# Packed attention with a routed MLP: token order of the key probabilities, the value load, and the queue that loads tau

## The chip, the cores and the metric

The kernel runs on one core of a Trainium2 chip. The metric is the device time of one execution in microseconds; less is better. The kernel before was run three times: 432.28 us in the median, 431.61 to 433.13. All times below are microseconds (us) unless marked ns.

## The reference

Eight batches of eight heads, 576 tokens of width 64. Per head, 32 pack queries `p` attend to the keys and values, and the tokens' own queries `q` then attend to the 32 packed rows. The result, 512 wide per token, goes through a mixture of eight experts of which each token uses one.

```python
def sm_attn(qq, kk, vv):
    s = scale * np.matmul(qq, kk.transpose(0, 1, 3, 2))
    s = s - np.max(s, axis=-1, keepdims=True)
    a = np.exp(s)
    a = a / (np.sum(a, axis=-1, keepdims=True) + 1e-09)
    return np.matmul(a, vv)
p_packed = sm_attn(p, k, v)              # 32 x 576 scores per head
out = sm_attn(q, p_packed, p_packed)     # 576 x 32 scores per head
...
logits = xn @ en.T / tau                 # x and the embeddings, each divided by its norm
expert_idx = np.argmax(logits, axis=1)
...
h = np.maximum(x[mask] @ w1[e], 0.0)
out[mask] = gate_w[mask, None] * (h @ w2[e])
```

## The kernel before

The batches go through one after the other, and two of them overlap: while TensorE does the expert MLP of batch b (`ffn`: lines 930, 958 and 976), pieces of the attention of batch b + 1 are put in between (`att1`, `att2`, `route`, `gates`). The order is written out by hand: `PLAN` says for batch 0 which piece follows each step of the MLP, and from batch 1 on a fixed rule advances the next batch's generator once per step. Each engine works through its own list in that order. Batch 0 has a start of its own, `begin`, with nothing to overlap it: it loads p, the embeddings, keys, values, queries and tau, does the first attention and guesses one expert for the whole batch; w1 and w2 of that expert are loaded after the guess (`load_w1`, `load_w2`). A loop at the end handles tokens that the guess misses.

The parts that the change touches:

- **Keys and queries.** A head's 576 tokens lie as 32 partitions of 18 neighbouring tokens each. `load_whole` (line 189, batch 0) loads four heads in one DMA, `load_nat` (line 174, later batches) two heads in four DMAs of 32 partitions. `flip` turns them in blocks of 32 x 32 on VectorE, so that column 32 n + i of `kt` is token 18 i + n. For queries that is one instruction (line 289). For keys it is three (lines 284 to 286), which also permute the blocks n. Each group of four heads has two flips at the start, one for each half of the width, and each later batch has four flips of keys and four of queries. A flip in `begin` is followed by `quarters` (line 237), the scores of that group.
- **Key softmax.** `key_max` (line 344, VectorE) and `key_exp` (line 349, ScalarE) make 128 x 576 probabilities `p1` of a group of four heads from PSUM; `p1` has the columns in the order of the scores. `p1_turn` (line 364) turns them on TensorE in five pieces, four of 128 columns and one of 64, each a weight load of the piece and a matmul with the identity; `p1_evac` copies the result out, and `pack_values` (line 384) multiplies by the values.
- **Values.** `load_v` (line 200) loads four heads. Partition 32 a + i holds tokens 18 i + n for the run of n that `RUNS` gives to the band a, five or four of them, so that piece c of `p1` meets the same tokens. Each band is a DMA of its own: 32 partitions, four heads, 1280 or 1024 bytes at a time.
- **tau.** One number, copied to 128 partitions of `itau` by a DMA of GpSimd's software queue (line 1096), issued behind the other loads in the program. Its reciprocal (line 1137) scales the logits.
- **Embeddings.** `embeddings` is a generator whose steps (norms by a Newton rsqrt, partly on VectorE, mostly on GpSimd) `begin` advances between its own.

Tiles of keys, queries and values share six buffers (`nat`). SP issues nearly all loads and stores, in program order.

Of the kernel before, what the change touches and what calls it, by code (L numbers as in the profile page):

```python
# [13 lines left out]
AF = mybir.ActivationFunctionType  # L14
# [3 lines left out]
P = 128  # L18
HB = 4
# [4 lines left out]
def kernel(  # L24
# [12 lines left out]
    nc = tc.nc  # L37
    B, H, S, D = q.shape
# [3 lines left out]
    NPR = H // 2  # L42
    NF = F // P
    HS = S // 2
    NCB = S // 32
# [23 lines left out]
    for h in range(HB):  # L69
        nc.vector.memset(pairs[32 * h : 32 * h + 32, h // 2 : h // 2 + 1], 1.0)  # L70
        for g in range(NG):
            at = (h ^ g) % 2
# [47 lines left out]
    itau = cp.tile([P, 1], F32, name="itau")  # L120
# [64 lines left out]
    def load_whole(src, g):  # L185

        t = sb.tile([P, NC5 * HB * D], F32, name="nat", tag="nat", bufs=6)[:, : NCB * D]
        s = src[0, g * HB : (g + 1) * HB].rearrange("h (i c) d -> h i (c d)", c=NCB)
        nc.sync.dma_start(t, s.rearrange("h i w -> (h i) w"))
        return t  # L190


    RUNS = ((0, 5), (5, 5), (10, 4), (14, 4))

    def load_v(b, g):
        t = sb.tile([P, NC5 * HB * D], F32, name="nat", tag="nat", bufs=6)
        t = t.rearrange("p (h w) -> p h w", h=HB)
        s = v[b, g * HB : (g + 1) * HB].rearrange("h (i c) d -> i h (c d)", c=NCB)
        for a, (at, n) in enumerate(RUNS):
            nc.sync.dma_start(  # L200
                t[32 * a : 32 * a + 32, :, : n * D], s[:, :, at * D : (at + n) * D]
            )
        return t.rearrange("p h (c d) -> p h c d", c=NC5)

    def load_p(b, queue=nc.sync):
# [9 lines left out]
    def rows(c):  # L215
        return P if c < 4 else 64
# [56 lines left out]
        nc.scalar.copy(dst[0], src)  # L273
        eng.tensor_tensor(out=dst[1], in0=src, in1=dst[0].bitcast(F32), op=ALU.subtract)

    def flip(t, key, e=0):

        kt = sb.tile([P, S], F32, name="kt", tag="kq", bufs=8)
        t = t.rearrange("p (c e d) -> p c e d", e=2, d=32)[:, :, e]
        if key:  # L280

            ko = kt[:, :512].rearrange("p (n a i) -> p a n i", a=4, i=32)
            ti = t[:, :10].rearrange("p (a n) d -> p a n d", a=2)
            nc.vector.transpose(ko[:, :2], ti[:, :, :4])
            nc.vector.transpose(ko[:, 2:], t[:, 10:].rearrange("p (a n) d -> p a n d", a=2))
            nc.vector.transpose(kt[:, 512:].rearrange("p (a i) -> p a i", i=32), ti[:, :, 4])
        else:

            nc.vector.transpose(kt.rearrange("p (n i) -> p n i", i=32), t)  # L289
        return kt  # L290

    def packers(x, pn):

        x.pw = sm.tile([P, NPR, 32], F32, name="pw", tag="pw", bufs=1)
        nc.vector.tensor_scalar_mul(pn, pn, SCALE)
        nc.vector.transpose(
            x.pw.rearrange("p r j -> p (r j)"), pn.rearrange("p r d -> p (r d)")
        )

    def keys(x, nat, pn):  # L300

        packers(x, pn)
        yield
        for r in range(NPR):
            x.kT[r] = flip(nat(r), True)
            yield


# [30 lines left out]
    def s1_view(x, g):  # L339
        return x.s1[g].rearrange("p (f s) -> p f s", f=2)[:, :, :HS]  # L340
# [5 lines left out]
    def key_exp(x, g):  # L346
        x.p1[g] = sb.tile([P, S], F32, name="p1", tag="p1", bufs=2)
        x.sums[g] = sm.tile([P, 1], F32, name="sums", tag="sums")
        nc.scalar.activation(
            x.p1[g].rearrange("p (f s) -> p f s", f=2), s1_view(x, g), AF.Exp, bias=x.mx[g],  # L350
            accum_out=x.sums[g],
        )

    def key_sum(x, g):
# [6 lines left out]
    def p1_turn(x, g, pt, pl):  # L361
        for c in range(NC5):
            r = rows(c)
            nc.tensor.transpose(  # L364
                (pt[:r, c * P : (c + 1) * P] if c < 4 else pl[:r, :P]),
                x.p1[g][:, c * P : c * P + r],
                ident,
            )

    def p1_evac(x, g, pt, pl, w=512, spare=None):  # L370

        x.p1T[g] = sb.tile([P, NC5, P], F32, name="p1T", tag=spare or "p1T", bufs=NF if spare else 2)
        t = x.p1T[g][:, 0:4].rearrange("p a b -> p (a b)")
        if w:
            nc.scalar.copy(t[:, :w], pt[:, :w])
        if w < 512:
            nc.vector.tensor_copy(t[:, w:], pt[:, w:512])
        nc.vector.tensor_copy(x.p1T[g][:64, 4], pl[:64, :P])
# [27 lines left out]
    def pair_rows(x, g, pt):  # L406
        x.pp2[g] = masked(x, g, pt, mask2[g], 2, "pp2")

    def packed_rows(x, g, pt):
        nc.scalar.mul(x.ppf[:, g, :D], pt[:, 0:D], x.rinv[g])  # L410
# [6 lines left out]
    def pack_tiles(x):  # L417
        x.T = x.Tq = sm.tile([P, NG * P], F32, name="T", tag="T", bufs=1)
        x.ppf = sb.tile([P, NG, XW], F32, name="ppf", tag="ppf", bufs=2)
# [15 lines left out]
    def att1(x, nat, tight=False):  # L435

        def queries():
            for r in range(NPR):
                x.qT[r] = flip(nat(NPR + r), False)
                yield  # L440

        turned = []

        def turn(g):
            turned.append(pb.tile([P, 1024], F32, name="pt", tag="pb"))
            p1_turn(x, g, turned[g], turned[g][:, 512:])

        def evac(g, w=512):
            p1_evac(x, g, turned[g], turned[g][:, 512:], w)

        def values():
            pt = pb.tile([P, 1024], F32, name="pt", tag="pb")
            for g in range(NG):
                pack_values(x, g, nat(2 * NPR + g), pt[:, g * D : g * D + D])
            return [pt[:, g * D : g * D + D] for g in range(NG)]

        def pack():
            pack_tiles(x)
            if not tight:
                yield  # L460
            for g in range(NG):
                turn(g)
            for g in range(NG):
                evac(g, 0 if tight and g else 512)
                if not tight:
                    yield
            if tight:
                yield
            pts = values()
            if not tight:  # L470
                yield
            for g in range(NG):
                pair_rows(x, g, pts[g])
            if not tight:
                yield
            pu = ps.tile([P, 512], F32, name="pu", tag="pf")
            if tight:
                for g in range(NG):
                    packed_rows(x, g, pts[g])
                yield  # L480
            for g in range(NG):
                pair_turn(x, g, pu)
            if not tight:
                yield
            (nc.scalar.copy if tight else nc.vector.tensor_copy)(x.T, pu[:, 0 : NG * P])
            if tight:
                yield
            else:
                for g in range(NG):
                    packed_rows(x, g, pts[g])  # L490
                yield from idle(2)
            pt = ps.tile([P, 512], F32, name="pu", tag="pf")
            row_logits(x, pt)
            if not tight:
                query_scores(x)
                yield
            logits_out(x, pt, nc.scalar.copy if tight else nc.vector.tensor_copy)
            yield

        key_scores(x)  # L500
        if tight:
            x.queries = queries()
        yield
        if tight:
            for g in range(NG):
                key_max(x, g)
            yield
            for g in range(NG):
                key_exp(x, g)
                key_sum(x, g)  # L510
                yield
            yield from pack()
            return
        for g in range(NG):
            key_max(x, g)
            yield
            key_exp(x, g)
            key_sum(x, g)
            yield
        yield from alternate(pack(), queries())  # L520
# [563 lines left out]
    def begin():  # L1084
# [3 lines left out]
        x = bat[0]  # L1088
        emb_gen = embeddings()
        pn = sm.tile([P, NG, D], F32, name="pn4", tag="pn")  # L1090
        nc.scalar.dma_start(pn, p[0].rearrange("(g h) j d -> (h j) g d", g=NG))
        next(emb_gen)
        kn = [load_whole(k, g) for g in range(NG)]
        vn = [load_v(0, g) for g in range(NG)]
        qn = [load_whole(q, g) for g in range(NG)]
        nc.gpsimd.dma_start(itau, tau.broadcast_to([P, 1]))

        def bank():
            return ps.tile([P, 512], F32, name="pf", tag="pf")
# [20 lines left out]
        for g in range(NG):  # L1120
            x.s1[g] = turn_bank()
            for e in range(2):
                kt = flip(kn[g], True, e)
                for hf in range(2):
                    quarters(x.s1[g], pw[:, 1, g, e], kt, lambda c: head(g, c), hf, hf, e)
            next(emb_gen)
            if g == 0:
                next(emb_gen)
        prefetch(1)
        key_max(x, 0)  # L1130
# [76 lines left out]
        for g in range(NG):  # L1207
            at = NG * 2 * D + g * NCB * D
# [180 lines left out]
    with tc.If(n_rest > 0):  # L1389
        with tc.For_i(0, B, 1) as b:  # L1390
            nb = nc.values_load(rest_i[0:1, ds(b, 1)], min_val=0, max_val=S)
            with tc.If(nb > 0):
                x = Batch()
                pn = load_p(b)
                nat = lambda i: load_nat(b, i)
# [96 lines left out]
```

## Time and profile before

| what | value |
|---|---|
| median of three runs | 432.28 us |
| the profiled execution | 434.17 us |
| its span, from the first instruction to the last | 432.5 us |
| TensorE matmuls busy (PE) | 416.7 us, 96% |
| weight loads busy (PEld; they overlap PE) | 349.6 us, 81% |
| VectorE busy (DVE) | 311.9 us, 72% |
| ScalarE busy (ACT) | 217.5 us, 50% |
| GpSimd busy (POOL) | 139.5 us, 32% |
| DMA, mean | 204 GB/s |

The profile is of one execution. In the rows further down, a row of the timeline has the start in us, the busy time in us, the engine, the line, the operation with out<-in and the shapes, and in brackets how long the engine had been idle and what ended that. SPq, ACTq and POOL rows with DMA_DIRECT2D are the issue of a DMA, not its transfer.

### The profile page before, as it was taken

The page shows a single profiled execution, that of the slowest core. Times are in us where ns is not written, and L with a number is a line of the kernel's source. Part 1 is how long each engine was busy: PE and PEld are TensorE (multiplying, and loading weights), DVE is VectorE, ACT ScalarE, POOL GpSimd, SP SyncE. Part 2 cuts the span into 40 slices and gives each one's busy share as a digit, 9 for nine tenths or more (in the row PEclk, how much of TensorE's full clock was granted, in tenths as well). Part 3 has the DMA queues.
Part 4 walks back from the last instruction along what each step waited for, and adds up shares of the span by engine and source line. Part 5 has one row for each costly group of instructions (what it writes and reads, how often), then busy time and mean ns, then how long its engine had stood idle before and what let it go on. Part 6 is the DMA issues. An engine that isn't in the chain of part 4 may idle for free.

```text
span 432.5 us, 12608 instructions
## 1 busy us (share of the span) xinstructions
PE 416.7 (96%) x4802; PEld 349.6 (81%) x4803; DVE 311.9 (72%) x980; ACT 217.5 (50%) x652; POOL 139.5 (32%) x187
## 2 busy tenths in 40 slices
PE   8789999999999999999999999999999999999993
PEld 6535879669887989869896889869896899869983
DVE  4477658878987689768897689868897589646320
ACT  1437715666435844366534744367434754456300
POOL 1438754343212514044222514044132424035000
PEclk9999999999999999999999999999999999999998
DMA  6989979886899479855998468965799504641032
GB/s 197 275 251 292 262 221 263 256 207 163 246 347 266 119 217 320 299 141 150 247 378 230 108 185 264 334 177 149 225 335 270 134 20 143 249 82 29 2 64 54
DMA packets 47908, 88.36 MB, mean 204 GB/s; under 512 B 10904, under 2 KB 29400, under 8 KB 47840
## 3 DMA queue, kind: packets, MB, share of 16 engines
q1 hardware_dynamic: 39456, 57.83, 49.9%
q0 software_dynamic: 8000, 29.43, 19.9%
q8 instruction: 40, 0.66, 0.7%
q10 hardware_dynamic: 384, 0.21, 0.2%
q14 instruction: 28, 0.23, 0.2%
HBM read 78.00 MB, written 9.44 MB: 202 GB/s over the span
## 4 chain that ended last, share of the span: by engine, by line
PE 81%; DMA 8%; DVE 5%; ACT 3%; issue 1%; SPq 1%; DVEq 0%; ACTq 0%
PE pf L958 24%; PE pf L930 21%; PE pf L976 19%; PE pt L259 3%; PE pt L688 3%; PE pt L848 3%; DMA w1t<-in_moe_w 3%; PE pt L384 2%; DMA nat<-in_q 2%; DMA nat<-in_v 2%; PE pt L364 2%; DMA nat<-in_k 2%; ACT scr L706 1%; ACT gt L785 1%; DVE G L862 1%
## 5 line engine op out<-in xcount | busy, mean ns | idle before, releaser
L824 POOL TENSOR_TENSOR w2s<-w2r,w2s 128x512 fp32r<-128x512 f32 x64 | 81.8, 1286 | 132.7 <-ACT w2s L823 129.0
L958 PE MATMUL pf<-hT,w2s 128*128 128x320 f32 x768 | 120.6, 312 | 0.0
L958 PEld LDWEIGHTS pf<-hT,w2s 128*128 128x128 f32 x768 | 113.0, 188 | 4.3 <-issue 3.3
L930 PE MATMUL pf<-AT,G 128*128 128x288 f32 x720 | 104.4, 299 | 0.3 <-DVE G L862 0.2
L930 PEld LDWEIGHTS pf<-AT,G 128*128 128x128 f32 x720 | 97.5, 188 | 5.5 <-ACT hT L932 2.3
L976 PE MATMUL pf<-w2s,hT 128*128 128x512 f32 (+1 forms) x408 | 94.9, 385 | 0.0
L976 PEld LDWEIGHTS pf<-w2s,hT 128*128 128x128 f32 x408 | 72.0, 188 | 20.6 <-issue 5.9
L933 DVE SCALAR_TENSOR_TENSOR hT<-pf,hT 128x288 fp32r<-128x288 f32 x128 | 56.3, 446 | 23.7 <-ACT hT L932 23.7
L932 ACT ACTIVATE hT<-pf 128x288 fp32r<-128x288 f32 x128 | 51.4, 415 | 34.9 <-PE pf L930 34.1
L706 ACT ACTIVATE scr<-pt 128x256 f32<-128x256 f32 (+1 forms) x80 | 29.7, 378 | 40.6 <-DVE lg L702 40.6
L823 ACT CAST w2s<-w2r 128x512 fp32r<-128x512 f32 x64 | 38.7, 624 | 3.4 <-issue 3.4
L799 POOL DMA_DIRECT2D w1t<-in_moe_w x14 | 10.7, 768 | 78.2 <-DVE st L588 73.5
L785 ACT COPY gt<-gate 32x2 f32<-32x2 f32 (+1 forms) x128 | 24.6, 192 | 6.5 <-DVE gate L770 4.2
L862 DVE TENSOR_TENSOR G<-pt,G 128x512 fp32r<-128x512 f32 x28 | 18.7, 688 | 12.6 <-ACT G L861 12.6
L1267 DVE STREAM_TRANSPOSE ot<-pf 128x320 f32<-128x320 f32 x32 | 16.0, 499 | 13.6 <-PE pf L958 11.4
L861 ACT CAST G<-pt 128x512 fp32r<-128x512 f32 x28 | 15.7, 588 | 18.0 <-DVE G L862 14.4
L609 ACT CAST AT<-at 128x576 fp32r<-128x576 f32 x16 | 10.8, 673 | 25.3 <-DVE at L606 25.3
L591 ACT ACTIVATE st<-st 128x576 f32<-128x576 f32 (+1 forms) x17 | 11.2, 658 | 23.3 <-issue 19.4
L702 DVE TENSOR_REDUCE lg<-pt 128x8 f32<-128x32 f32 (+1 forms) x80 | 11.5, 175 | 14.9 <-PE pt L688 10.1
L289 DVE STREAM_TRANSPOSE kt<-nat 128x576 f32<-128x576 f32 x28 | 21.2, 762 | 0.0
L1250 ACT ACTIVATE o<-pf,gate 128x512 f32<-128x512 f32 (+1 forms) x17 | 11.4, 668 | 18.7 <-issue 14.3
L807 POOL DMA_DIRECT2D w2r<-in_moe_w x28 | 19.8, 711 | 0.0
(179 smaller groups left out, 496.0 us busy)
## 6 DMA issues: line engine op xcount, KB each, us to landing
nat<-in_k SPq DMA_DIRECT2D x112, 140.0 KB, 3.6
nat<-in_q SPq DMA_DIRECT2D x112, 140.0 KB, 4.4
w1t<-in_moe_w POOLq DMA_DIRECT2D x14, 1024.0 KB, 8.5
w2r<-in_moe_w POOLq DMA_DIRECT2D x28, 512.0 KB, 12.1
nat<-in_v SPq DMA_DIRECT2D x32, 160.0 KB, 3.9
out<-ot SPq DMA_DIRECT2D x28, 160.0 KB, 3.5
nat<-in_v SPq DMA_DIRECT2D x32, 128.0 KB, 3.7
out<-o SPq DMA_DIRECT2D x62, 64.0 KB, 1.7
```

The lines of the kernel that those rows point to most:

```text
L289: nc.vector.transpose(kt.rearrange("p (n i) -> p n i", i=32), t)
L706: nc.scalar.activation(scr[:r], v[:, :, :D], AF.Square, accum_out=sss[:r, m, c : c + 1])
L785: copy(dst[32 * a : 32 * a + 32, k : k + HB * (n - 1) + 1 : HB], src[32 * k : 32 * k + 32, NCT : NCT + n],)
L807: queue.dma_start(t, w2e[:, 2 * i : 2 * i + 2, :])
L823: nc.scalar.copy(hi, raw)
L824: eng.tensor_tensor(out=lo, in0=raw, in1=hi.bitcast(F32), op=ALU.subtract)
L862: nc.vector.tensor_tensor(out=x.G[:, 1, g, fs], in0=src, in1=x.G[:, 0, g, fs].bitcast(F32), op=ALU.subtract,)
L930: nc.tensor.matmul(pf[:, :HS], w, r, start=(n == 0), stop=(n == len(ops) - 1))
L932: nc.scalar.activation(hT[:, 0, f, cs], pf[:, :HS], AF.Relu)
L933: nc.vector.scalar_tensor_tensor(out=hT[:, 1, f, cs], in0=pf[:, :HS], scalar=0.0, in1=hT[:, 0, f, cs].bitcast(F32), op0=ALU.max, op1=ALU.s ...
L958: nc.tensor.matmul(pf[:, : S - TL], x.w2s[f][:, m, mt * P : mt * P + P], hT[:, a, f, TL:], start=(n == 0), stop=(n == len(ops) - 1),)
L976: nc.tensor.matmul(pf[:, :w], hT[:, a, f, c * P : (c + 1) * P], x.w2s[f][:, m, at : at + w], start=(f == 0 and i == 0), stop=(f == NF - 1 ...
```

## The change

```diff
-    RUNS = ((0, 5), (5, 5), (10, 4), (14, 4))
-
     def load_v(b, g):
+
         t = sb.tile([P, NC5 * HB * D], F32, name="nat", tag="nat", bufs=6)
         t = t.rearrange("p (h w) -> p h w", h=HB)
-        s = v[b, g * HB : (g + 1) * HB].rearrange("h (i c) d -> i h (c d)", c=NCB)
-        for a, (at, n) in enumerate(RUNS):
-            nc.sync.dma_start(
-                t[32 * a : 32 * a + 32, :, : n * D], s[:, :, at * D : (at + n) * D]
-            )
+        s = v[b, g * HB : (g + 1) * HB]
+        body = s[:, : 4 * P].rearrange("h (i c) d -> i h (c d)", c=4)
+        nc.sync.dma_start(t[:, :, : 4 * D], body)
+        nc.sync.dma_start(t[:64, :, 4 * D :], s[:, 4 * P :].rearrange("h i d -> i h d"))
...
-    def flip(t, key, e=0):
+    def flip(t, e=0):
...
-        if key:
-
-            ko = kt[:, :512].rearrange("p (n a i) -> p a n i", a=4, i=32)
-            ti = t[:, :10].rearrange("p (a n) d -> p a n d", a=2)
-            nc.vector.transpose(ko[:, :2], ti[:, :, :4])
-            nc.vector.transpose(ko[:, 2:], t[:, 10:].rearrange("p (a n) d -> p a n d", a=2))
-            nc.vector.transpose(kt[:, 512:].rearrange("p (a i) -> p a i", i=32), ti[:, :, 4])
-        else:
-
-            nc.vector.transpose(kt.rearrange("p (n i) -> p n i", i=32), t)
+        nc.vector.transpose(kt.rearrange("p (n i) -> p n i", i=32), t)
...
         nc.scalar.activation(
-            x.p1[g].rearrange("p (f s) -> p f s", f=2), s1_view(x, g), AF.Exp, bias=x.mx[g],
-            accum_out=x.sums[g],
+            x.p1[g].rearrange("p (i f n) -> p f n i", f=2, n=NCB // 2),
+            s1_view(x, g).rearrange("p f (n i) -> p f n i", i=32),
+            AF.Exp, bias=x.mx[g], accum_out=x.sums[g],
         )
...
                 (pt[:r, c * P : (c + 1) * P] if c < 4 else pl[:r, :P]),
-                x.p1[g][:, c * P : c * P + r],
+                x.p1[g][:, c : 4 * P : 4] if c < 4 else x.p1[g][:, 4 * P :],
                 ident,
...
         next(emb_gen)
+        nc.scalar.dma_start(itau, tau.broadcast_to([P, 1]))
         kn = [load_whole(k, g) for g in range(NG)]
         vn = [load_v(0, g) for g in range(NG)]
         qn = [load_whole(q, g) for g in range(NG)]
-        nc.gpsimd.dma_start(itau, tau.broadcast_to([P, 1]))
...
-                kt = flip(kn[g], True, e)
+                kt = flip(kn[g], e)
...
             next(emb_gen)
-            if g == 0:
+            if g:
                 next(emb_gen)
```

Every key flip is one instruction, and the scores keep the block order. `key_exp` writes them in token order instead: the 32 scores of a block go to places 18 floats (72 bytes) apart. Piece c < 4 of `p1_turn` takes the columns c, c + 4, ... up to 511, a step of 16 bytes; the last takes tokens 512 to 575 as they lie. The values of tokens 0 to 511 come by one DMA, four neighbouring tokens (1024 bytes) per partition and head, those of the last 64 by a second, 256 bytes each. tau goes by ScalarE's queue, ahead of the keys in the program, and the second step of the embeddings follows the flips of the second group.

The order of the instructions on three engines, at the start of the program. First VectorE, at the key flips of batch 0 (`kt`) and the first two steps of the embeddings' rsqrt (`rq_i`):

```order
+L278 STREAM_TRANSPOSE kt<-nat 128x576 x4
 L88 TENSOR_SCALAR rq_i<-ess 8x1
-L284 STREAM_TRANSPOSE kt<-nat 128x2x4x32
-L285 STREAM_TRANSPOSE kt<-nat 128x2x4x32
-L286 STREAM_TRANSPOSE kt<-nat 128x64
-L284 STREAM_TRANSPOSE kt<-nat 128x2x4x32
-L285 STREAM_TRANSPOSE kt<-nat 128x2x4x32
-L286 STREAM_TRANSPOSE kt<-nat 128x64
 L92 TENSOR_SCALAR rq_i<-rq_i 8x1
```

Twelve instructions become four (six of the twelve stand just above this piece), and L88 now stands behind all of them instead of between the two groups.

Then SP's loads at the start, with the values of both groups between keys and queries:

```order
 L189 DMA nat<-in_k 128x1152 x2
-L200 DMA nat<-in_v 32x4x320 x2
-L200 DMA nat<-in_v 32x4x256 x2
-L200 DMA nat<-in_v 32x4x320 x2
-L200 DMA nat<-in_v 32x4x256 x2
+L199 DMA nat<-in_v 128x4x256
+L200 DMA nat<-in_v 64x4x64
+L199 DMA nat<-in_v 128x4x256
+L200 DMA nat<-in_v 64x4x64
 L189 DMA nat<-in_q 128x1152 x2
 L174 DMA nat<-in_k 32x1120 x7
```

Four loads stand ahead of the queries in place of eight; the seven loads behind them are batch 1's first keys. Later batches lose two loads per tile of values in the same way.

And ScalarE's queue, where the DMAs of p, the embeddings and now tau stand ahead of the first table load:

```order
 L126 DMA emb_sb<-in_moe_expert_emb 8x512
+L1083 DMA itau<-in_moe_tau 128x1
 L129 ACT_TABLE_LOAD
 L129 ACTIVATE esq,ess<-emb_sb 8x512
```

The row of itau is new there; in GpSimd's list the one between the two steps that make the identity is gone.

## Rows read from the trace of the kernel before

**Rows 1.** Windows view: stretch; its length; busy PE, PEld, DVE, ACT, POOL; clock, DMA.

```profile
0.00:19.00 19.00, 15.82 (x211) 12.28 (x212) 9.72 (x70) 6.70 (x16) 7.01 (x29) 1.00 0.85 236
19.00:36.00 17.00, 14.05 (x91) 5.94 (x90) 9.18 (x22) 7.24 (x16) 5.14 (x7) 1.00 0.86 249
36.00:44.00 8.00, 7.63 (x68) 4.78 (x67) 7.25 (x23) 5.02 (x12) 7.64 (x6) 1.00 1.08 299
44.00:88.00 44.00, 42.41 (x634) 34.87 (x634) 33.17 (x104) 23.53 (x87) 21.73 (x38) 1.00 0.91 251
88.00:94.00 6.00, 4.95 (x51) 2.98 (x49) 4.66 (x11) 3.62 (x7) 1.36 (x2) 1.00 0.91 227
142.47:191.66 49.19, 49.19 (x598) 42.16 (x593) 39.66 (x120) 26.29 (x81) 14.82 (x18) 1.00 0.77 230
```

**Rows 2.** Timeline of the start: tau's issue, value loads, key flips and scores.

```profile
1.47 0.72 POOL L1096 DMA_DIRECT2D itau<-in_moe_tau  x1 [0.36 <-issue]
...
1.83 7.13 SPq L200 DMA_DIRECT2D nat<-in_v  x8
...
5.62 0.40 DVE L284 STREAM_TRANSPOSE kt<-nat 128x256 f32<-128x256 f32 x1
...
6.79 2.14 PE L237 MATMUL pt<-kt,pw 32*32 32x288 f32 x32
...
8.65 0.45 DVE L284 STREAM_TRANSPOSE kt<-nat 128x256 f32<-128x256 f32 x1 [1.38 <-DMA nat<-in_k]
...
9.48 2.14 PE L237 MATMUL pt<-kt,pw 32*32 32x288 f32 x32 [0.54 <-DVE kt L285]
```

**Rows 3.** DMA view, 0 to 20 us: 40 slices of 0.5 us; tau's issue to landing.

```profile
GB/s 0 0 0 65 147 175 321 420 353 434 406 184 0 13 215 298 212 231 210 227 222 209 215 248 232 244 258 359 433 396 404 381 197 251 260 206 302 259 212 207
...
itau<-in_moe_tau POOLq DMA_DIRECT2D x1, 0.5 KB, 7.1
```

**Rows 4.** Timeline of batch 0's first expert matmuls, line 890.

```profile
24.17 3.09 PE L890 MATMUL pf<-w1t,tw 64*32 64x512 f32 x16
...
29.60 1.05 PE L890 MATMUL pt<-w1t,tw 64*32 64x512 f32 x4
...
31.57 0.15 PEld L890 LDWEIGHTS pt<-w1t,tw 64*32 64x32 f32 x8 [1.83 <-DMA w1t<-in_moe_w]
31.57 1.91 PE L890 MATMUL pt<-w1t,tw 64*32 64x512 f32 x12 [0.92 <-DMA w1t<-in_moe_w]
```

**Rows 5.** Groups by line: busy us, mean ns of one; idle before, releaser.

```profile
L289 DVE STREAM_TRANSPOSE kt<-nat 128x576 f32<-128x576 f32 x28 | 21.2, 762 | 0.0
...
L344 DVE TENSOR_REDUCE mx<-pt 128x1 f32<-128x576 f32 x16 | 11.9, 748 | 0.7 <-PE pt L237 0.7
...
L702 DVE TENSOR_REDUCE lg<-pt 128x8 f32<-128x32 f32 x64 | 9.2, 177 | 13.9 <-PE pt L688 10.1 <-ACT scr L706 3.7
...
L364 PEld LDWEIGHTS pt<-ident,p 128*128 128x128 f32 x64 | 7.5, 140 | 1.8 <-POOL rq_t L102 0.9 <-ACT p L349 0.9
```

**Rows 6.** Timeline: two query flips in a row; the last key flip ahead of G.

```profile
53.09 1.43 DVE L289 STREAM_TRANSPOSE kt<-nat 128x576 f32<-128x576 f32 x2
...
88.06 0.40 DVE L284 STREAM_TRANSPOSE kt<-nat 128x256 f32<-128x256 f32 x1
...
88.83 0.65 DVE L862 TENSOR_TENSOR G<-pt,G 128x512 fp32r<-128x512 f32 x1
...
92.91 1.17 PE L259 MATMUL pt<-kt,pw 64*32 64x288 f32 x24 [0.85 <-DVE G L862]
```

**Rows 7.** Timeline of batch 1: the second Exp and the turns.

```profile
47.78 0.74 ACT L349 ACTIVATE p<-pt,mx 128x576 f32<-128x576 f32 x1
...
48.20 1.25 PE L364 MATMUL pt<-ident,p 128*128 128x128 f32 x10
```

**Rows 8.** Timeline of the steady part: the second Exp and the turns.

```profile
147.68 0.74 ACT L349 ACTIVATE p<-pt,mx 128x576 f32<-128x576 f32 x1 [0.38 <-DVE mx L344]
...
149.08 1.25 PE L364 MATMUL pt<-ident,p 128*128 128x128 f32 x10
```

More of the change, by code (lines that the diff above doesn't have):

```diff
@@ L304, in keys @@
         for r in range(NPR):
-            x.kT[r] = flip(nat(r), True)
+            x.kT[r] = flip(nat(r))
             yield
@@ L438, in queries @@
             for r in range(NPR):
-                x.qT[r] = flip(nat(NPR + r), False)
+                x.qT[r] = flip(nat(NPR + r))
                 yield
```

## The prediction

> **What bounds the kernel now.** I read the stretches first. From 142.47 to 191.66 us, one whole batch of the steady part, TensorE is busy 49.19 of 49.19 us [rows 1]; that period repeats for batches 2 to 7. There, an instruction taken from VectorE, ScalarE or a queue is worth nothing, and every nanosecond added to TensorE's own stream is paid. Only before 94 us does TensorE stand still: 3.18 us idle in 0 to 19, 2.95 in 19 to 36, 0.37 in 36 to 44, 1.59 in 44 to 88 and 1.05 in 88 to 94, 9.1 us in all [rows 1]. A gain can come from there alone.
>
> Next I read the start in the timeline. The flip of the second key tile begins at 8.65 us, after VectorE waited 1.38 us for its load, and TensorE's scores of that group at 9.48; the scores of the first group were done at 6.79 + 2.14 = 8.93 [rows 2]. The DMA view says why the load is late. Its 0.5 us slices from 1.5 to 6.0 us add up to 1.25 MB, which is both key tiles (2 x 576 KB) with p and the embeddings; then two slices show 0 and 13 GB/s, though value loads had been issued from 1.83 us on [rows 2, 3]. tau, the one load that GpSimd's software queue has in flight, was issued at 1.47 and landed 7.1 us later, at 8.57 [rows 2, 3], about when the key tile was released. I read the hole as the price of that queue's first packets. After it the values move at 209 to 298 GB/s (mean 229, slices of 7.0 to 12.5), and the queries, which are spread over 128 partitions, at about 404 (14.0 to 16.0) [rows 3].
>
> Last, the first expert matmuls: the second half of them starts at 29.60, waits 1.83 us for w1 in front of its last twelve, and ends at 31.57 + 1.91 = 33.48 [rows 4]. The first half took 3.09 us in one piece.
>
> **The change part by part.**
>
> *tau by ScalarE's queue.* The hole goes, if it is tau's. The second key tile then lands between 6.0 (its bytes were through) and 8.63 (no change); I take about 7. VectorE's flips of the first group run from 5.62 [rows 2] to about 7.1, so those of the second end by 8.5, and TensorE starts its scores at 8.93 instead of 9.48: **0.55 us** gained, no more, since it is busy until then. The bounds are 0 and 0.55. ScalarE issues one more DMA, in time in which it would wait for the embeddings; GpSimd loses the issue's 0.72 us [rows 2], for which nobody waits. The first step of the embeddings' rsqrt, one short instruction, moves behind VectorE's last flip; the rest of that chain on GpSimd ends long before its result is used.
>
> *Values by two DMAs per tile.* At the start SP issues four in place of eight, so the queries behind them go out earlier. 1.18 MB at 229 GB/s is 5.2 us, at the queries' 404 it is 2.9; for the 256-byte pieces of the last 64 tokens I add 0.5 and take 3.4. With the hole that empties the queues about 2.7 us earlier (bounds 0 and 3.3) before w1 is issued. w1's wait of 1.83 us at 31.57 [rows 4] then ends: the second half starts at 29.60 - 0.55 = 29.05, takes the first half's 3.09 and ends at 32.14, 1.34 before 33.48. So the loads add **0.8 us** to the 0.55 (bounds 0 and 1.8). What is late next is VectorE, which is busy 7.25 of 8 us in 36 to 44 [rows 1].
>
> *Keys turned in one step.* Three pieces take 88.83 - 88.06 = 0.77 us from start to the next instruction; of two single flips of the queries the second starts 1.43 - 0.76 = 0.67 after the first [rows 5, 6]. That is 0.10 less per flip. At the start it buys nothing: the scores began 0.83 us after the flip's first piece [rows 2], when two of the three were done, and the whole flip takes 0.76. In 36 to 44 four flips stand between the ReLU halves for which TensorE waits: 4 x 0.10 = **0.4 us**. At 88 four flips stand ahead of the weight splits (88.83), for whose last TensorE waits 0.85 us at 92.91 [rows 6]: another **0.4 us**. Bounds 0 and 0.8 in all. In the steady part: nothing.
>
> *Exp written in token order.* 32 neighbouring scores go to places 72 bytes apart. No row here shows ScalarE writing so. Below: 0. Above: its 0.74 us again [rows 7]. The nearest row is VectorE's reduction that reads PSUM at a step of 1 KB, 177 ns for 32 values; against 748 ns for 576 neighbouring values [rows 5] that is (748 - 177) / 544 = 1.05 ns per value and no sign of a second slot (at two per value it would be about 210). I take 0. On the path lie the second Exp of the start and the two of batch 1: there the second ends at 48.52, the ten turns run from 48.20 [rows 7], and a longer Exp is paid. From batch 2 on the second Exp ends at 148.42 and its turns come about half-way through 149.08 to 150.33 [rows 8], so up to about 0.8 us is hidden there.
>
> *The turns' weights at a step of 16 bytes.* Four of five weight loads of a turn (line 364) take every fourth column. The load takes 140 ns [rows 5], the ten stand 1.25 us with the last one's tail [rows 8], about 0.11 us each; TensorE has nothing else to do beside them. Below: 0. Above: a second pass over the 128 columns, 0.11 more each. Nearest is the same strided reduction; I take 0, with less trust than anywhere else here, for PSUM is not SBUF and VectorE is not the weight path.
>
> The Trainium skill speaks against this ("Advanced Engine Details and Errata", SBUF Cachelines): an access needs at least two hits on a 16-byte line to run at full rate, and a line per access costs a penalty. It gives no size. By it both last terms would be above zero, which is the first rival below; no run so far shows either.
>
> **Sum.** 0.55 + 0.8 + 0.4 + 0.4 = 2.15, say 2.2 us. The profiled execution took 434.17 us (span 432.5, and 1.67 around it), so 432.0; the median of the runs, 432.28, lies 1.9 below it, and I carry that over: **430.1 us**.
>
> **The rivals.**
>
> *Slower: the strided weights pace the turns.* In the steady part TensorE never waits, so the extra is paid whole: 8 loads in each of batches 1 to 7, and 4 of batch 0 (the second group's) are 60. At 0.11 us that is 6.5, less the 2.2: **436.6 us**. It decides from 2.2 / 60 = 0.037 us per load. For it: a turn does nothing but load and stream 128 columns, so nothing covers a slower load. Against it: the strided reduction pays nothing. By the rule of the Trainium skill named above ("Advanced Engine Details and Errata", SBUF Cachelines) the turns would go this way.
>
> *The Exp alone pays.* At 0.74 more, three on the path cost 2.2 and the gain is gone: **432.3 us**. For it: ScalarE is the busy one when batch 1 turns its keys. Against: the same reduction, and a smaller price leaves part of the gain.
>
> *The start does not move.* The hole is not tau's, or w1 lands as late because of its own 2 MB: then only the 0.8 us of the flips can be left, and part of it if TensorE waits for w1 anyway: **431.8 us**. For it: that software packets end the hole is inferred from the two landings alone. Against: the value loads had long been issued.
>
> **Chances.** The forecast 0.45, the weights 0.33, the Exp 0.11, the unmoved start 0.11. A measurement of this kernel tells about 0.3%, 1.3 us, from no change. The forecast is faster in 0.41 and within 1.3 us in 0.04; the weights are slower in 0.32 and within in 0.01; the Exp faster in 0.03 and within in 0.08; the unmoved start faster in 0.01, within in 0.09, slower in 0.01. That makes 0.45 faster, 0.22 the same, 0.33 slower. The range goes from 428.6 (all upper bounds of the gains: 0.55 + 1.8 + 0.8 = 3.2, and 0.5 for what follows) to 436.6, the first rival with its full price. The forecast's own range is 428.6 to 431.5.
>
> **What would show it.** Right: no empty DMA slice at 6 us; the second flip at about 7 and the scores of group two at 8.93; no wait for w1 before the last twelve; single flips at 0.67; Exp still 0.74 and the weight load 140 ns; steady period still 49.18. Wrong: a period above 49.18 with longer weight loads at the turns (first rival), Exp near 1.2 or more with a gap of TensorE at 48 us (second), or a second key tile still at 8.6 (third).

## The result and the profile after

The changed kernel takes **436.51 us**, median of 6 runs (435.22 to 438.49), against 432.11 for the kernel before beside it: ratio 1.0096, 95% interval 1.0072 to 1.0120. It is slower by about 4.2 us. The forecast was 430.1, so its sign is wrong; the time lies at the upper end of the range, 0.1 us from the price of the first rival, and the experiments show that it got there by another way. The profiled execution of the kernel after, 435.22 us, is 1.3 below its median, while that of before is 1.9 above its own; the two traces are therefore only 1.0 us of span apart (433.5 and 432.5), and what one part costs has to come from medians or from traces beside each other.

The stretches of the kernel after, in the windows view (columns as in rows 1; its batch 2 begins at 140.12):

```profile
0.00:19.00 19.00, 15.60 (x223) 12.34 (x228) 9.72 (x62) 8.36 (x17) 6.47 (x28) 1.00 0.82 251
19.00:36.00 17.00, 15.98 (x96) 7.37 (x85) 12.00 (x28) 9.04 (x20) 8.38 (x9) 1.00 0.95 303
36.00:44.00 8.00, 8.00 (x83) 6.49 (x82) 5.71 (x12) 5.75 (x14) 7.01 (x6) 1.00 1.09 289
140.12:189.73 49.61, 49.61 (x597) 42.31 (x591) 39.03 (x112) 27.09 (x81) 14.81 (x18) 1.00 0.75 228
```

Up to 44 us TensorE does more than before: 19 to 36 holds 15.98 us of its work in place of 14.05 [rows 1]. Between these two traces the start did get shorter: batch 2 begins at 140.12 in place of 142.47. How much of these 2.35 us is the change and how much the one execution of before is taken up further down. The steady period got longer, 49.61 in place of 49.19 [rows 1].

The groups by line name the two instructions that changed their price:

```profile
L338 ACT ACTIVATE p<-pt,mx 128x576 f32<-128x576 f32 x16 | 21.4, 1340 | 6.4 <-DVE mx L333 6.4
...
L354 PEld LDWEIGHTS pt<-ident,p 128*128 128x128 f32 x64 | 9.0, 206 | 3.2 <-ACT p L338 1.6 <-POOL ery L112 1.5
```

The Exp (line 338, 349 before) takes 1340 ns where it took 743: 0.60 us more, eighty per cent of a second pass. A turn's weight load takes 206 where it took 140 [rows 5].

The timeline of the start, where the forecast's gain was to come from:

```profile
1.22 5.23 PE L1099 MATMUL pf<-fill 128*128 128x128 f32 x26 [1.22 <-DVE mask L68]
...
5.67 2.72 DVE L278 STREAM_TRANSPOSE kt<-nat 128x576 f32<-128x576 f32 x4
6.46 3.46 PE L235 MATMUL pt<-kt,pw 32*32 32x288 f32 x64
9.46 1.34 ACT L338 ACTIVATE p<-pt,mx 128x576 f32<-128x576 f32 x1 [3.49 <-DVE mx L333]
...
10.78 1.34 ACT L338 ACTIVATE p<-pt,mx 128x576 f32<-128x576 f32 x1
...
12.18 0.86 PE L354 MATMUL pt<-ident,p 128*128 128x128 f32 x5 [0.40 <-ACT p L338]
```

The second key tile is no longer late: four flips run in one piece from 5.67, and the 64 score matmuls of both groups in one piece from 6.46, right behind the 26 warm-up matmuls of line 1099 (before: 6.79 and, after a break, 9.48 [rows 2]). Then the longer Exp, twice in a row, holds up the second group's turns until 12.18.

In the steady part the timeline of the kernel after shows what stands behind an Exp on ScalarE:

```profile
143.00 1.34 ACT L338 ACTIVATE p<-pt,mx 128x576 f32<-128x576 f32 x1
...
144.18 0.71 ACT L922 ACTIVATE hT<-pf 128x288 fp32r<-128x288 f32 x2
...
145.67 0.45 DVE L923 SCALAR_TENSOR_TENSOR hT<-pf,hT 128x288 fp32r<-128x288 f32 x1
145.79 1.34 ACT L338 ACTIVATE p<-pt,mx 128x576 f32<-128x576 f32 x1 [0.39 <-DVE mx L333]
146.17 0.83 PEld L920 LDWEIGHTS pf<-AT,G 128*128 128x128 f32 x6 [0.20 <-DVE hT L923]
```

The ReLU copies of line 922 empty the PSUM banks of the expert matmuls (line 920). The first pair starts 1.18 us after the Exp did; the forecast had looked only at when the turns need the probabilities [rows 8], not at these copies. VectorE's half of the ReLU (line 923) comes later with them, and TensorE's weights wait for it at 146.17.

### The profile page after: what moved, and what is told of

Read it like the earlier page. It is cut to its first block, busy times and chain, and to the rows that moved or that the text cites. A ratio compares the mean times of both kernels' runs of the same rounds, so it can differ in the third digit from the quotient of the medians.

```text
span 433.5 us, 12505 instructions
## 1 busy us (share of the span) xinstructions
PE 417.9 (96%) x4802; PEld 350.2 (81%) x4803; DVE 307.4 (71%) x916; ACT 224.2 (52%) x652; POOL 138.9 (32%) x186
## 4 chain that ended last, share of the span: by engine, by line
PE 88%; DVE 5%; ACT 4%; DMA 1%; issue 1%; SPq 0%; DVEq 0%; ACTq 0%
PE pf L948 24%; PE pf L920 21%; PE pf L966 21%; PE pt L257 3%; PE pt L678 3%; PE pt L838 3%; PE pt L374 2%; PE pt L354 2%; ACT p L338 2%; PE pf L1099 1%; PE pf L899 1%; PE pf L880 1%; ACT scr L696 1%; DVE hT L923 1%; DMA nat<-in_q 1%
## 5 line engine op out<-in xcount | busy, mean ns | idle before, releaser
L920 PE MATMUL pf<-AT,G 128*128 128x288 f32 x720 | 106.2, 300 | 0.2 <-DVE hT L923 0.2
L278 DVE STREAM_TRANSPOSE kt<-nat 128x576 f32<-128x576 f32 x60 | 44.6, 757 | 0.0
L338 ACT ACTIVATE p<-pt,mx 128x576 f32<-128x576 f32 x16 | 21.4, 1340 | 6.4 <-DVE mx L333 6.4
```

The source lines that it names most:

```text
L338: nc.scalar.activation(x.p1[g].rearrange("p (i f n) -> p f n i", f=2, n=NCB // 2), s1_view(x, g).rearrange("p f (n i) -> p f n i", i=32), ...
L920: nc.tensor.matmul(pf[:, :HS], w, r, start=(n == 0), stop=(n == len(ops) - 1))
```

## The experiments

**The two steps taken out, one at a time and together.** Three versions of the kernel after:

```
# e1: the Exp writes p1 in the order of its scores
-            x.p1[g].rearrange("p (i f n) -> p f n i", f=2, n=NCB // 2),
+            x.p1[g].rearrange("p (f n i) -> p f n i", f=2, i=32),
# e2: the turns take neighbouring columns
-                x.p1[g][:, c : 4 * P : 4] if c < 4 else x.p1[g][:, 4 * P :],
+                x.p1[g][:, c * P : c * P + r],
# e3: both
```

> The changed kernel with the Exp writing its columns as they lie (the same walk over blocks of 32, no 72-byte steps); the turns keep their 16-byte steps, so probabilities are paired with values of other tokens. Exp theory (the strided write holds ScalarE 0.6 us longer per Exp, and in the steady part the ReLU copies behind it make TensorE wait): Exp back to about 0.74 us, steady period 49.18 + 0.08 = 49.26 us, time 4 to 5 us under the changed kernel, near 431 to 432. Weight theory (the turns' strided loads are what costs): Exp may shorten, but the period stays 49.6 and the time stays at 436 to 437.

> The changed kernel with the turns taking neighbouring columns again; the Exp keeps its strided write, so probabilities are paired with values of other tokens. Exp theory: weight load back to 140 ns, Exp still 1.34 us, period about 49.5, time 0.5 to 1 us under the changed kernel, near 435.5 to 436. Weight theory: period 49.2, time near 430 to 432.

> The changed kernel without either stride (probabilities paired with values of other tokens): what is left is the single flips, the two value loads and tau's queue. If the start gains what was forecast: period 49.18, time 2.2 us under the kernel before, near 429.9; as the trace of the changed kernel shows w1 no longer waited for and the second half of the first expert matmuls ending at 30.2 in place of 33.5, up to 4 us, 428. If the gains of the start do not reach the end, 431.5 to 432.5.

Measured: e1 432.85 us (ratio to before 1.0008, 0.9986 to 1.0030), e2 435.68 (1.0083, 1.0057 to 1.0110), e3 432.34 (0.9993, 0.9971 to 1.0016). The Exp's step is worth 436.51 - 432.85 = 3.7 us, the turns' step 0.5 (e1 against e3) to 0.8 (e2 against the kernel after). In e1 the Exp takes 742 ns and the steady period 49.24; in e2 ten turns take 1.09 us in the chain and not 1.17, and the period stays at 49.50. That settles it between the first two rivals: the Exp pays, the turns hardly. But e3, which keeps every gain of the change and neither cost, is no faster than the kernel before.

**tau's queue alone.** The kernel before with one line moved, run in two jobs:

```
+        nc.scalar.dma_start(itau, tau.broadcast_to([P, 1]))
         kn = [load_whole(k, g) for g in range(NG)]
...
-        nc.gpsimd.dma_start(itau, tau.broadcast_to([P, 1]))
```

> The kernel before with tau alone moved to ScalarE's queue. If the empty 0.9 us of all DMA engines at 6 us was the price of the software queue's first packets: no hole, the second key tile lands at about 7, the scores of group two start at 8.93, and the time is 0.5 to 1.5 us under the kernel before (430.6 to 431.6). If the hole has another cause: it stays and the time is within 0.3 us of the kernel before.

> The kernel before with tau on ScalarE's queue alone, as in e4_tau_only (430.84 us), once more beside e9_reads_pad. Theory A: 430.8 again, ratio to the kernel before 0.996. If e9_reads_pad comes out at 431.2 the two differ by 0.4, less than a measurement of this kernel tells from no change; if the gain of e4_tau_only was chance, 432.2.

Measured: 430.84 (0.9963, 0.9941 to 0.9985) and 431.13 (0.9960, 0.9946 to 0.9975), beside medians of the kernel before of 432.47 and 432.99; by the ratios 1.6 to 1.7 us faster, both times. The hole was tau's: in the DMA view of e4, 0 to 20 us in slices of 0.5, no slice is empty at 6 us any more (rows 3 have 0 and 13 GB/s there).

```profile
GB/s 0 0 0 65 138 212 274 413 376 419 424 349 175 159 280 246 218 210 235 211 199 240 263 174 323 396 424 396 421 308 224 206 260 302 264 239 217 212 269 215
```

Where the 1.6 us stand, in e4's timeline and then in e10's:

```profile
6.81 3.38 PE L237 MATMUL pt<-kt,pw 32*32 32x288 f32 x64
...
11.94 0.76 PE L364 MATMUL pt<-ident,p 128*128 128x128 f32 x5 [0.41 <-ACT p L349]
```

```profile
6.38 3.75 PE L237 MATMUL pt<-kt,pw 32*32 32x288 f32 x64
...
11.87 0.77 PE L364 MATMUL pt<-ident,p 128*128 128x128 f32 x5 [0.59 <-ACT p L349]
```

In the chain of the kernel before those five turns start at 13.37, so 1.4 to 1.5 us are won there. The start of the scores is not what was won: it follows the warm-up and varies (6.79 before, 6.81 in e4, 6.38 in e10). The 64 in one piece end at 10.19 and 10.13, in place of 9.48 + 2.14 = 11.62 with a break between two pieces. A second trace with tau on GpSimd's queue bears this out: e11 below is the kernel before up to its probes at 350 us, its flip of the second key tile starts at 8.47 and its five turns at 13.19. Its DMA view has no empty slice, though, only one of 78 GB/s at 6 us; the late tile is common to the two traces, the complete stop is not.

**The other gains, one at a time on top of tau's queue.** e5 is e4 with the two-DMA `load_v` of the change, e6 is e4 with its single `flip`.

> The kernel before with tau on ScalarE's queue (e4_tau_only, 430.84 us) and, of the rest of the change, only the value loads as two DMAs; the probabilities are then paired with values of other tokens. What is to be told apart is why e3_both_flat (432.34) stands 1.5 us above e4_tau_only. Theory A, the closing code: the loads cost nothing in the work, but SP's program is shorter by two DMAs a load, and its last instructions after the branch over the fallback then lie across a fetch of instructions; from the start of the last ACT o to the end of the span the profile shows 7.9 us (6.35 in e4_tau_only), and the time is 432.2. Theory B, the loads themselves: pieces of 512 and 128 bytes land later (4.3 us after the issue against 3.8), a batch's value turns wait for them; the close stays at 6.35, the steady period is over 49.17 or the turns of batch 3 start after 146.9, and the time is 432.0 to 432.5. Theory C: neither, 430.0 to 430.8.

> The kernel before with tau on ScalarE's queue (e4_tau_only, 430.84 us) and, of the rest of the change, only the single flip of a key tile; the probabilities are then paired with values of other tokens. Theory A, the closing code: SP's program is that of e4_tau_only, the close stays at 6.35 us after the start of the last ACT o, and the time is 430.0 to 430.8, the flips being worth 0 to 0.8 us. Theory B, the flips take the 1.5 us back (a flip of 128x576 holds VectorE 677 ns without a break, and what is queued behind it stands): steady period over 49.17, time 431.5 to 432.5.

The sizes in e5's theory B are not those of the rows: the loads that landed 4.3 us after their issue are of 512 KB in pieces of 1024 bytes (the kernel after), those of 3.8 us are of 128 KB (e4).

Measured: e5 432.78 (1.0022, 1.0001 to 1.0043), e6 430.94 (0.9968, 0.9953 to 0.9983). The flips are worth nothing that can be told; the 0.8 us forecast for them are 0.2%, about what these intervals leave open. The loads lose all that tau's queue won, and the chain of waits shows where: not in the work. Here are the spans and, from the chain of waits (start, duration, what), the last activation of e10 and then of e5:

```profile
core 0 of [0], span 429.4 us
...
423.03 0.47 ACT o L1250
```

```profile
core 0 of [0], span 431.1 us
...
423.10 0.47 ACT o L1248
```

The last outputs are made at the same time, 423.03 and 423.10, and the turns of batch 3 start at 146.47 in both chains, although e5's value loads land later (4.8 to 4.9 us after the issue in the median, 3.8 to 3.9 in e4). Then e10 closes in 6.4 us and e5 in 8.0. In these 8.0 SP branches over the fallback for leftover tokens and clears its semaphores; in the trace of e5 these clears follow each other at about 0.1 us, but one stands 1.62 us behind the one before it (427.75 to 429.37), and an 8 KB packet of the queue that fetches instructions starts at 427.87, just behind that gap's beginning. The kernel after has the same gap (430.36 to 431.79), e4 has none. Such a packet alone proves nothing: one starts 0.6 to 0.9 us behind the first of these clears in the traces without a gap too (427.58 in e4). What speaks for the fetch is the end of the gap. In the six traces that have one (the kernel after, e1, e2, e3, e5, e7) SP goes on 1.48 to 1.57 us after that packet's start, as it does behind the branch itself (427.13 in e5, 1.59 us after an 8 KB packet at 425.54). SP's program is shorter by two DMAs for each value tile, so the same closing code lies elsewhere.

**Moving the closing code.** If its place is the cause, code that never runs must matter. In the fallback eight of the output stores are written four times over, 24 DMA instructions more on SP and nothing else changed:

```
-                for c in range(NCT):
+                for c in 4 * list(range(NCT)):
                     for a in range(HB):
                         nc.sync.dma_start(
```

> The kernel after with 24 DMA instructions of SP more in the fallback for leftover tokens, which the program branches over and never runs; nothing that runs is changed, but the code behind the fallback stands elsewhere. Theory A, the closing code: the 24 instructions move the border of the instruction fetch out of SP's last clears; from the start of the last ACT o to the end of the span 6.4 to 6.6 us (7.9 in the kernel after), time 435.1. Theory B, the longer close comes from the work itself (stores that land later, the order of queues): 7.9 us, time 436.5.

The close is short again. First the kernel after, then e8:

```profile
core 0 of [0], span 433.5 us
...
425.65 0.47 ACT o L1240
```

```profile
core 0 of [0], span 435.4 us
...
429.07 0.47 ACT o L1240
```

7.9 us became 6.3. The median, 436.09 (1.0090, 1.0073 to 1.0107), is lower by 0.4 only and its interval overlaps that of the kernel after; its six runs spread over 2.3 us, and the profiled one, the longest, was 3.4 us behind at the end of its first expert matmuls (33.64 against 30.27). So the trace shows that the place of the code decides the length of the close (that a fetch is what SP waits for is inferred from the packets), and the time of this run leaves open what it is worth; e9 below bears on that.

**Reading with a step in place of writing with one.** The Exp can walk the tile in the order of its output. Then it writes p1 without a step and reads the scores in PSUM 128 bytes apart. e7 is the kernel after with that; e9 adds e8's padding.

```
-            x.p1[g].rearrange("p (i f n) -> p f n i", f=2, n=NCB // 2),
-            s1_view(x, g).rearrange("p f (n i) -> p f n i", i=32),
+            x.p1[g].rearrange("p (i f n) -> p i f n", f=2, n=NCB // 2),
+            s1_view(x, g).rearrange("p f (n i) -> p i f n", i=32),
```

> The kernel after with the Exp walking its tile in the order of its output: it writes p1 without a step and reads the scores from PSUM with a step of 128 bytes; the result is that of the kernel after. Theory A, the price of the Exp is on the side that writes SBUF: L338 takes 743 to 800 ns as before, steady period 49.2, time 432.8. Theory B, any step costs as much, on whichever side: L338 takes 1340 ns or more, steady period 49.6 or more, time 436.5. Between: a smaller price of the reads, L338 some 1000 ns, time 434 to 435.

> The kernel after with both repairs: the Exp writes p1 without a step and reads PSUM with a step of 128 bytes (e7_exp_reads, 432.67 us), and 24 DMA instructions of SP more in the fallback that never runs (e8_pad_close, whose close was 6.3 us after the start of the last ACT o, 7.9 without). Theory A, both costs are what they were taken for and add up: L338 743 ns, steady period 49.26, close 6.4, time 431.2 (432.67 less 1.5). Theory B, the close is worth nothing in the time of an execution (e8_pad_close came out 0.4 below the kernel after, within its spread): 432.6. Below 430.8 it would beat e4_tau_only.

Measured: e7 432.67 (1.0018, 1.0004 to 1.0033), e9 431.44 (0.9960, 0.9941 to 0.9980); the two intervals, each to the kernel before measured beside it, lie apart, so the close counts in the time too. How much is less sure: the medians differ by 1.2 us, the ratios by 0.6% or 2.5 us, and the gap is 1.5. e7's Exp:

```profile
L338 ACT ACTIVATE p<-pt,mx 128x576 f32<-128x576 f32 x16 | 11.9, 743 | 7.0 <-DVE mx L333 7.0
```

The whole price is gone with the step in PSUM. Since e7 and the kernel after differ in this alone, their chains of waits show where 0.60 us per Exp are paid. The kernel after, then e7:

```profile
30.27 0.59 ACT g L890
...
50.28 0.34 DVE pp L386
...
97.66 1.17 PE pt L354 x10
...
147.24 1.17 PE pt L354 x10
...
425.65 0.47 ACT o L1240
```

```profile
29.90 0.59 ACT g L890
...
49.11 0.35 DVE pp L386
...
96.09 1.16 PE pt L354 x10
...
145.34 1.17 PE pt L354 x10
...
422.37 0.47 ACT o L1240
```

The lead of e7 grows from 0.37 us at the first experts to 1.17 in batch 1, 1.57 at the turns of batch 2, 1.90 at those of batch 3 and 3.28 at the end. The last step, 1.38, is four periods of 49.61 against 49.26. Here is the windows' row for e7's batch 2, and from the two chains, the kernel after first, the one piece of that period whose length differs by more than 0.01 us (line 920, beside the two Exps):

```profile
138.57:187.83 49.26, 49.26 (x597) 42.26 (x591) 39.24 (x112) 26.39 (x81) 14.83 (x18) 1.00 0.77 230
```

```profile
141.16 6.08 PE pf L920 x42
```

```profile
139.61 5.73 PE pf L920 x42
```

The whole 0.35 us of a period are lost in these 42 expert matmuls, and of the waits listed for TensorE's weights in the period only the one for line 923 is not in e7's list.

**The price by the step.** Probes of 128x576 between two SBUF tiles, behind the kernel's own work in the program (the scheduler ran them at 350 us).

> The kernel before with a row of probes behind the last store's work: Exp of one SBUF tile of 128x576 into another, written flat (L1385), with a step of 2, 4, 6, 8, 9, 16, 18 and 32 elements (L1386 to L1393), and read with a step of 18 but written flat (L1394); VectorE copies written with a step of 18, read with a step of 18, and flat (L1395 to L1397); TensorE turns of 128 columns with a step of 1, 2 and 4 and of 64 columns with a step of 8 (L1399 to L1402). Theory A, the price is ScalarE's write alone, and there from some step on: L1385 and L1394 near 740 ns, L1392 (step 18, 72 bytes) near 1340, VectorE's three copies equal. Theory B, any step over 1 costs the same: L1386 to L1393 all near 1340. For the turns: weight loads of 140 ns flat and 206 with a step of 4, the others between or above. The time itself says nothing.

The groups by line of ScalarE, VectorE and the weight loads:

```profile
L1394 ACT ACTIVATE src<-dst 128x576 f32<-128x576 f32 x1 | 1.3, 1282 | 0.0
L1392 ACT ACTIVATE dst<-src 128x576 f32<-128x576 f32 x1 | 1.3, 1281 | 0.0
...
L1387 ACT ACTIVATE dst<-src 128x576 f32<-128x576 f32 x1 | 1.2, 1230 | 0.0
...
L1393 ACT ACTIVATE dst<-src 128x576 f32<-128x576 f32 x1 | 1.2, 1175 | 0.0
...
L1386 ACT ACTIVATE dst<-src 128x576 f32<-128x576 f32 x1 | 0.7, 738 | 0.0
L1385 ACT ACTIVATE dst<-src 128x576 f32<-128x576 f32 x1 | 0.7, 685 | 0.7 <-DVE rq_h L97 0.7
```

```profile
L1395 DVE COPY dst<-src 128x576 f32<-128x576 f32 x1 | 0.7, 706 | 10.1 <-ACT src L1394 10.1
L1396 DVE COPY src<-dst 128x576 f32<-128x576 f32 x1 | 0.7, 700 | 0.0
...
L1397 DVE COPY dst<-src 128x576 f32<-128x576 f32 x1 | 0.5, 459 | 0.0
```

```profile
L1401 PEld LDWEIGHTS pf<-ident,dst 128*128 128x128 f32 x1 | 0.2, 210 | 0.0
L1400 PEld LDWEIGHTS pf<-ident,dst 128*128 128x128 f32 x1 | 0.2, 198 | 0.0
...
L1399 PEld LDWEIGHTS pf<-ident,dst 128*128 128x128 f32 x1 | 0.1, 138 | 0.0
```

Theory B falls, and of A only one half stands: that there is a step from which it costs. Each figure is one instruction of one execution. ScalarE pays from a step of 16 bytes (L1387, 1230 ns) and hardly at 8 (L1386, 738); beyond 16 bytes the price stays, 1167 to 1282 up to 128 bytes (L1393). And it is not the side of the write: reading SBUF at 72 bytes (L1394) costs what writing at 72 does (L1392). So e7 is fast because its step lies in PSUM, not because it reads.

## Why the prediction was wrong

By its own steps, in us against the kernel before:

| step | forecast | measured | from |
| --- | --- | --- | --- |
| tau by ScalarE's queue | -0.55 | -1.6 | e4, e10 |
| values by two DMAs, in the work | -0.8 | 0 | e5: last outputs at 423.10, e10 at 423.03 |
| values by two DMAs, SP's close | none | +1.6 | e5, e8, e9 |
| single flips | -0.8 | 0, within 0.2% | e6 against e4, e10 |
| Exp in token order | 0 | +3.4 to 3.8 | e7, e1 |
| turns' weights | 0 | +0.5 to 0.8 | e1 against e3, e2 |

With the middle of each range the sum is about +4.2, and 1.0096 is 4.15. This is not wholly a test: the Exp and the turns were measured by taking them out of the changed kernel. What is independent is that the first four rows come to 0, as e3 does (0.9993).

**The failed step is the Exp.** It was priced at 0 by "the nearest row", a VectorE reduction at a step of 1 KB [rows 5]. That row was in another memory: it reads PSUM, and e7 shows that ScalarE, too, pays nothing for a step there (743 ns at 128 bytes). The step of the change lies in SBUF, and there ScalarE pays 0.60 us. The text said so of the weights ("PSUM is not SBUF") and did not say it of the Exp. The Trainium skill ("Advanced Engine Details and Errata", SBUF Cachelines) states what the probes then showed: two hits on a 16-byte line are enough, one is not (738 ns at two values per 16 bytes, 1230 at one). On TensorE's weight load two were not enough (198 ns at 8 bytes, 138 flat). The prediction had quoted that rule, gave it a rival, and set it aside in the sum.

**Second, "hidden there" was asked of the wrong successor.** The second rival had the Exp's mechanism and even its upper bound about right (0.74, measured 0.60), but counted three Exps and took the steady part as free up to 0.8 us, because the turns come later [rows 8]. The next instructions on ScalarE are the ReLU copies for which TensorE waits; 0.35 us a period got through, 1.7 in all from the turns of batch 2 on.

**The first rival met the time by luck and not by the cause.** A weight load did get 0.066 us longer (140 to 206), but ten turns only 0.08 (1.09 to 1.17 in the chain): the load was measured, its place in the pipeline was not. In the probes four loads of different steps start 0.11 us apart all the same.

**Of the three gains of the start only one was there to win.** tau's queue was sized by the moment at which TensorE had finished the first group, as if both groups had to stay in two pieces; it gave three times the forecast.

The value loads' 0.8 us rested on the wait for w1 [rows 4], and that wait belonged to the execution, not to the kernel. (Its 1.83 us are the idle time of the weight loads; the matmuls idled 0.92.) e11, the same kernel up to 350 us, has no such wait of the matmuls: in its chain the second half of the first expert matmuls ends at 29.47 + 1.85 = 31.32, where the prediction read 33.48. The matmuls wait for w1 in the traces of before, e1, e3 and e6, by 0.8 to 1.0 us, and these four executions lie 1.1 to 1.9 us above their kernel's median; they do not in any trace at or below its median (the kernel after, e2, e4, e5, e7, e10). So the prediction read a gain off an execution 1.9 us above the median, and then took the 1.9 off once more, though 1.5 of it seem to lie in the start itself: e11's turns of batch 3 start at 147.77, those of before at 149.24. Of the 2.35 us by which the kernel after was ahead of before at batch 2, about 0.9 are then left to the change. e11 is one run, so these two figures are estimates. In e4 the second half ends at 28.13 + 1.85 = 29.98, 1.3 before e11, which is tau's gain again, and e7, with the value loads, starts the next step at 29.90, hardly sooner.

From 34.19 to 41.60 us e10's chain runs through a value load (7.41 us), and TensorE is busy 7.92 of 8 us in 36 to 44 there, so the flips had no wait left to shorten either. That the hole at 6 us was tau's, held right; so did the price of the single flips (2.72 us for four in a row).

**SP's close was in no term and in no rival.** It cancels the whole gain of tau's queue, which is why e3 came out at no change.

What stays open: whether the value loads cost a few tenths in the work. e5's ratio is 0.6% above e4's where its trace explains 1.6 us, 0.4%, and the table's 0 is read from single traces; in e5's chain a batch-2 value load lands late (6.07 us from issue at 96.15), as one does in e10 too (3.12 us from 98.98).

**The better kernel.** Both e4 (430.84 and 431.13, one line) and e9 (431.44) beat the kernel before, by 0.4%, and the changed one by 1.2 to 1.3%. They differ by less than a measurement tells.

## What to carry to other kernels

Take the price of an access with a step from a row with the same memory, the same engine and about the same step; where there is none, the bound, and not the row at hand, belongs in the sum. If a layout must be turned inside an instruction that reads PSUM and writes SBUF, put the step on the PSUM side. Before a wait is counted as a gain, look for it in a second execution, above all when the profiled one lies above the median. And ask of "hidden" which instruction stands next in that engine's own queue, and who waits for that one.

## What the runs showed of the hardware

- ScalarE on 576 values a partition in SBUF: 685 ns flat, 738 at 8 bytes, 1167 to 1282 from 16 to 128 bytes written, 1282 at 72 bytes read. VectorE's copy: 459 flat, 700 and 706 at 72 bytes. In PSUM, 128 bytes apart, ScalarE takes 743, as without a step.
- A weight load of 128 columns: 138 ns flat, 198 at 8 bytes, 210 at 16. There is no free step here, but little of it reaches the turns.
- Where the code behind a skipped branch lies is worth 1.6 us at the end: 24 instructions that never run took it away (7.9 to 6.3 us). The Trainium skill ("Runtime: NRT & Kernel Launch", Instruction fetch mechanics) says that a taken branch to a place outside the pages at hand waits for a fetch, and that crossing a block is mostly hidden. The first agrees: 2.7 us from SP's branch to its next instruction in e4, with an 8 KB packet 1.1 us behind the branch. If the gap 0.6 us behind the first clear is such a crossing, it was not hidden there: 1.4 to 1.7 us in six traces.
- With one 0.5 KB load on GpSimd's software queue the second key tile came late in both traces of such a kernel (its flip at 8.65 and 8.47, 7.25 in e4), and the kernel lost 1.6 us by it. All transfers stopped in one of the two only: 0 and 13 GB/s in two slices [rows 3], 78 at the lowest in e11.
